# DMA crossbar transposes in place of TensorE transposes in a diffusion transformer block, with the weight loads reordered around them

## The chip, the cores and the metric

The kernel runs on one core of a Trainium2 chip. Its engines are TensorE (PE, the matrix multiplier), VectorE (DVE), ScalarE (ACT), GpSimd (POOL) and SyncE (SP). In this kernel SP only issues loads and stores, and its queue keeps the order of the program. The granted clock is the share of TensorE's full speed that the chip let it run at, as the profile records it; L681 and the like are lines of the kernel's source. The metric is the device time of one execution in microseconds (us); lower is better.

## The reference, cut to what matters

The shapes are B = 2, N = 256 tokens each, D = 1152, two heads, FC width 4608, all in bf16.

```python
h = _layernorm(x) * (1 + scale_a) + shift_a
q, k, v = ...                                   # h @ wqkv
attn = _softmax(einsum('bqhd,bkhd->bhqk', q, k) * Dh ** (-0.5))
a = einsum('bhqk,bkhd->bqhd', attn, v).reshape(B, N, D) @ wo
x = x + gate_a * a
h2 = _layernorm(x) * (1 + scale_m) + shift_m    # "LN2"
m = _gelu(h2 @ w_fc1) @ w_fc2                   # "FC1", "FC2"
return x + gate_m * m
```

The scale, shift and gate vectors, called modulation rows and gate rows below, are computed from a second input with the weights `w_mod`.

The kernel's matmuls contract over the partition axis (the 128 rows of on-chip memory). So the probabilities must be transposed before they meet V ("PV"), and the normalised rows of LN2 before they meet the FC1 weights.

## The kernel before

A small list scheduler in the kernel orders the instructions of DVE, ACT and POOL by estimated priority. PE and SP keep the order in which the program names their work.

Four buffers matter. WFC2 holds all of the FC2 weights in four quarters of nine blocks. WFC1 has four slots, so groups 4 to 8 of the FC1 weights must wait until a slot has been read. XN2, the normalised rows of LN2, lies in the last bytes of the *last* WFC2 quarter: that quarter can't be loaded until the rows have been transposed.

```python
        WFC2 = sb(O_R, 4 * W1).rearrange("p (k f) -> p k f", k=JT)
        WFC1 = [wmat(o, 512) for o in (O_A, O_A + 9216, O_C, O_C + 9216)]
...
        XN2 = [sb(O_R + 4 * W1 - (i + 1) * 2304, 2304) for i in range(4)]
```

The transposes on PE write PSUM; DVE and ACT then copy them out, those of LN2 with scale and shift applied on the way:

```python
        def pt_transposes(b, h):
            idx = b * 2 + h
            bank = s_bank[(b, h)]
            S.unit("pe", 4 * c_mm(128), "PT_%d_%d" % (b, h))
            for kjt in range(2):
                for jq in range(2):
                    tr(ps16(bank, kjt * 256 + jq * 128, 128), PP[idx][:, jq, kjt * 128:(kjt + 1) * 128], IDENT)
            copy_on("dve" if b == 0 else "act", PTS[idx].rearrange("p j k -> p (j k)"), ps16(bank, 0, 512), 512, True, "PT_ev%d" % idx)
...
        def xn2_T(t):
            b = t // 2
            xn2 = XN2[t]
            S.unit("pe", KT * c_mm(128), "xn2T_%d" % t)
            slot = [ps16(7, kt * 128, 128) if kt < 4 else ps16(6, (kt - 4) * 128, 128) for kt in range(KT)]
            for kt in range(KT):
                tr(slot[kt], xn2[:, kt * 128:(kt + 1) * 128], IDENT)
            for kt in range(KT):
                o, dst = slot[kt], H2T[:, kt, t * 128:(t + 1) * 128]
                s1, s2 = SC1M[:, kt * 2 + b:kt * 2 + b + 1], SHM[:, kt * 2 + b:kt * 2 + b + 1]
                if kt < (4 if t < 2 else 6):
                    dve(335, lambda e, o=o, dst=dst, s1=s1, s2=s2: e.tensor_scalar(out=dst, in0=o, scalar1=s1, scalar2=s2, op0=ALU.mult, op1=ALU.add),
                        [o, s1, s2], [dst], "h2T_%d_%d" % (t, kt))
                else:
                    act(440, lambda e, o=o, dst=dst, s1=s1, s2=s2: e.activation(out=dst, in_=o, func=ACTF.Identity, scale=s1, bias=s2),
                        [o, s1, s2], [dst], "h2T_%d_%d" % (t, kt))
```

This is the order of the second half. Three quarters of WFC2 are queued before PV and WO, the last one after eight FC1 half-tiles; LN2 transposes are placed between matmuls at points where their rows are ready. An FC1 tile is 128 of the 4608 columns; the first F0 = 8 tiles are done for tokens 0 to 255 and later for 256 to 511, so that FC1 can start before the last rows are there.

```python
        for q4 in range(3):
            dma(WFC2[:, 9 * q4:9 * q4 + 9, :], wfc2_v[:, 9 * q4:9 * q4 + 9, :], 9 * P * D * 2, "ld_wfc2_%d" % q4, run=2304)
        for b in range(2):
            for h in range(2):
                pv(b, h)
        wo_tile(0)
        wo_tile(1)
        wo_tile(2)
        xn2_T(0)
        wo_tile(3, {2: lambda: xn2_T(1)})
        for f in range(0, 4):
            fc1_tile(f, 0, 256)
        xn2_T(2)
        for f in range(4, F0 - 2):
            fc1_tile(f, 0, 256)
        xn2_T(3)
        for f in range(F0 - 2, F0):
            fc1_tile(f, 0, 256)
        dma(WFC2[:, 27:36, :], wfc2_v[:, 27:36, :], 9 * P * D * 2, "ld_wfc2_3", run=2304)
        for f in range(F0):
            fc1_tile(f, 256, 256)
        for f in range(F0, JT):
            if f % 4 == 0 and f // 4 >= 4:
                wfc1_load(f // 4)
            fc1_tile(f, 0, 512)
```

## Time and profile before

| | before |
|---|---|
| median of the first 3 runs | 249.41 us (249.25 to 249.88) |
| span of the profiled execution | 247.4 us |
| PE busy | 241.7 us, 98% |
| granted TensorE clock | 1.0 |
| TensorE transposes that the change removes | 52, in 8 groups |

From the profile's page: the busy times of each engine; then PE, the granted clock and the DMA engines in 40 equal slices of the span, a digit being tenths; then the chain of waits (what was running, followed back from the end) by engine.

```profile
...
PE 241.7 (98%) x1827; PEld 149.5 (60%) x1827; DVE 69.9 (28%) x179; ACT 63.8 (26%) x129; POOL 19.6 (8%) x33
...
PE   6999999999999999999999999999999999999995
...
PEclk9999999999999999999999999999999999999999
DMA  6999989999999999999953660000000000000000
...
PE 94%; ACT 2%; DMA 2%; DVE 1%; issue 0%
...
```

PE has no slack: 98% busy, 94% of the chain, full clock. The DMA engines are nearly full for 20 slices (to about 124 us), half full for four more, while the last WFC2 quarter and the later FC1 groups come, and then empty. ACT and DVE, at about a quarter each, don't limit.

From the same chain in order of time (start, length, what; `L681` is the helper for transposes in this kernel): a group of four transposes of probabilities, and three groups of nine of LN2.

```profile
...
60.40 0.22 PE psum L681 x4
...
97.14 0.52 PE psum L681 x9
...
106.72 0.50 PE psum L681 x9
...
109.19 0.57 PE psum L681 x9
...
```

They cost 0.22 us and 0.50 to 0.57 us per group and lie on the chain (of the fourth LN2 group five of the nine, 0.45 us). That is the most by which the change can shorten PE's queue: 4 × 0.22 + about 2.1 = 3.0 us, 1.2%.

The busy time of each engine by stretches (start:end and length, then busy us and count per engine; the last three columns are granted clock, DMA share, GB/s):

```profile
...
core 0: us, PE busy (x) PEld busy (x) DVE busy (x) ACT busy (x) POOL busy (x), PEclk, DMA share, GB/s
90.00:118.00 28.00, 27.91 (x238) 21.68 (x237) 17.48 (x51) 16.86 (x35) 10.26 (x13) 1.00 1.05 386
118.00:126.00 8.00, 8.00 (x46) 4.28 (x44) 0.00 (x0) 2.55 (x6) 0.00 (x0) 1.00 1.01 326
126.00:134.00 8.00, 8.00 (x39) 3.63 (x38) 0.00 (x0) 2.44 (x5) 0.00 (x0) 1.00 0.48 153
...
```

While WO, LN2 and early FC1 run (90 to 118 us) PE is busy and the loads flow beside it at 386 GB/s: the WFC2 quarters are fetched for nothing there.

### The profile page before, as it was taken

The page shows a single profiled execution, that of the slowest core. Times are in us where ns is not written, and L with a number is a line of the kernel's source. Part 1 is how long each engine was busy: PE and PEld are TensorE (multiplying, and loading weights), DVE is VectorE, ACT ScalarE, POOL GpSimd, SP SyncE. Part 2 cuts the span into 40 slices and gives each one's busy share as a digit, 9 for nine tenths or more (in the row PEclk, how much of TensorE's full clock was granted, in tenths as well). Part 3 has the DMA queues.
Part 4 walks back from the last instruction along what each step waited for, and adds up shares of the span by engine and source line. Part 5 has one row for each costly group of instructions (what it writes and reads, how often), then busy time and mean ns, then how long its engine had stood idle before and what let it go on. Part 6 is the DMA issues. An engine that isn't in the chain of part 4 may idle for free.

```text
span 247.4 us, 4146 instructions
## 1 busy us (share of the span) xinstructions
PE 241.7 (98%) x1827; PEld 149.5 (60%) x1827; DVE 69.9 (28%) x179; ACT 63.8 (26%) x129; POOL 19.6 (8%) x33
## 2 busy tenths in 40 slices
PE   6999999999999999999999999999999999999995
PEld 2589954566656766798544444444566666666674
DVE  3742440555322679950000000000012222111112
ACT  4730340344301404984333222332000000000000
POOL 1300000000013167500000000000000000000000
PEclk9999999999999999999999999999999999999999
DMA  6999989999999999999953660000000000000000
GB/s 240 372 375 393 390 299 414 426 423 420 409 385 332 309 364 391 392 386 383 358 156 138 191 191 3 0 0 0 3 16 16 19 16 16 16 19 21 27 19 17
DMA packets 27644, 51.59 MB, mean 209 GB/s; under 512 B 1511, under 2 KB 15591, under 8 KB 26475
## 3 DMA queue, kind: packets, MB, share of 16 engines
q1 hardware_dynamic: 27216, 50.14, 56.0%
q0 software_dynamic: 384, 1.19, 1.5%
q8 instruction: 14, 0.23, 0.4%
q14 instruction: 3, 0.02, 0.0%
q10 hardware_dynamic: 27, 0.00, 0.0%
HBM read 50.14 MB, written 1.19 MB: 208 GB/s over the span
## 4 chain that ended last, share of the span: by engine, by line
PE 94%; ACT 2%; DMA 2%; DVE 1%; issue 0%
PE psum L678 92%; PE psum L681 2%; DMA arena<-in_x_dram 2%; ACT arena L1049 1%; ACT arena L1033 1%; ACT arena L731 1%; ACT arena L730 1%; DVE arena L744 0%; DVE arena L783 0%; DVE arena L1139 0%; DVE arena L732 0%; DVE arena L1140 0%; DVE arena L774 0%; DVE arena L734 0%
## 5 line engine op out<-in xcount | busy, mean ns | idle before, releaser
L678 PE MATMUL psum<-arena 128*128 128x384 bf16 (+7 forms) x1720 | 237.7, 305 | 1.8 <-POOL arena L701 1.4
L678 PEld LDWEIGHTS psum<-arena 128*128 128x128 bf16 (+1 forms) x1720 | 143.8, 97 | 91.0 <-issue 3.1
L1139 DVE TENSOR_TENSOR arena<-psum,arena 128x384 f32<-128x384 f32 (+3 forms) x14 | 7.0, 501 | 119.2 <-PE psum L678 119.2
L1059 ACT ACTIVATE arena<-psum 128x512 bf16<-128x512 f32 (+1 forms) x44 | 22.5, 522 | 42.6 <-PE psum L678 42.6
L673 ACT ACTIVATE arena<-psum 128x512 bf16<-128x512 f32 (+7 forms) x29 | 15.4, 553 | 36.2 <-PE psum L678 33.8
L675 DVE CAST arena<-psum 128x512 bf16<-128x512 f32 (+4 forms) x23 | 14.0, 621 | 32.1 <-PE psum L678 32.0
L1028 POOL TENSOR_TENSOR arena<-arena 128x384 f32<-128x384 f32 x12 | 11.0, 913 | 11.2 <-DVE arena L1027 10.0
L722 DVE BATCH_NORM_STATS2 arena<-arena 128x6 f32<-128x384 f32 (+1 forms) x18 | 9.5, 548 | 0.8 <-DMA arena<-in_x_dram 0.7
L681 PE MATMUL psum<-arena 128*128 128x128 bf16 (+2 forms) x107 | 7.8, 209 | 0.9 <-DMA arena<-in_c_dram 0.7
L681 PEld LDWEIGHTS psum<-arena 128*128 128x128 bf16 (+2 forms) x107 | 6.3, 97 | 3.7 <-DMA arena<-in_c_dram 1.6
L1033 ACT ACTIVATE arena<-arena 128x1152 bf16<-128x1152 f32 x4 | 5.4, 1353 | 9.5 <-DVE arena L1032 9.5
L1027 DVE TENSOR_TENSOR arena<-psum,arena 128x384 f32<-128x384 f32 x12 | 6.6, 548 | 3.2 <-PE psum L678 2.6
L1140 DVE TENSOR_TENSOR arena<-arena 128x384 bf16<-128x384 f32 (+3 forms) x14 | 7.0, 501 | 0.5
L1049 ACT ACTIVATE arena<-psum,arena 128x128 bf16<-128x128 bf16 x16 | 6.1, 460 | 3.2 <-PE psum L681 2.5
L659 POOL DMA_DIRECT2D dit_scratch<-arena x2 | 1.2, 629 | 61.3 <-DVE arena L675 61.3
L1046 DVE TENSOR_SCALAR arena<-psum,arena 128x128 bf16<-128x128 bf16 x20 | 5.5, 338 | 2.0 <-PE psum L681 1.8
L924 ACT ACTIVATE arena<-psum,arena 128x256 bf16<-128x256 f32 x8 | 3.7, 471 | 6.9 <-PE psum L678 5.4
L726 POOL TENSOR_TENSOR arena<-arena 128x1 f32<-128x1 f32 x6 | 3.3, 553 | 8.7 <-DVE arena L725 8.7
L887 ACT ACTIVATE arena<-arena 128x256 bf16<-128x256 bf16 x6 | 2.5, 496 | 4.3 <-DVE arena L881 4.3
L920 DVE TENSOR_REDUCE arena<-psum 128x2 f32<-128x512 f32 x4 | 2.8, 690 | 1.5 <-PE psum L678 1.5
L783 DVE TENSOR_SCALAR arena<-psum,arena 128x256 bf16<-128x256 bf16 x7 | 2.4, 349 | 2.7 <-PE psum L681 1.4
L928 DVE TENSOR_TENSOR arena<-arena 128x512 bf16<-128x512 bf16 x4 | 2.8, 688 | 0.1
(37 smaller groups left out, 30.9 us busy)
## 6 DMA issues: line engine op xcount, KB each, us to landing
arena<-in_w_mod_dram SPq DMA_DIRECT2D x3, 3456.0 KB, 25.9
arena<-in_w_fc_dram SPq DMA_DIRECT2D x9, 1152.0 KB, 8.6
arena<-in_w_fc_dram SPq DMA_DIRECT2D x4, 2592.0 KB, 20.7
arena<-in_wqkv_dram SPq DMA_DIRECT2D x18, 288.0 KB, 10.0
arena<-in_w_mod_dram SPq DMA_DIRECT2D x3, 864.0 KB, 13.1
arena<-in_wqkv_dram SPq DMA_DIRECT2D x1, 2592.0 KB, 10.0
arena<-in_wo_dram SPq DMA_DIRECT2D x1, 2592.0 KB, 39.7
arena<-in_w_mod_dram SPq DMA_DIRECT2D x3, 480.0 KB, 6.8
```

The costliest lines, as they stand in the source:

```text
L673: act(c_act(n), lambda e: e.activation(out=dst, in_=src, func=ACTF.Copy), [src], [dst], name)
L675: dve(c_dve_psum16(n) if psum16 else c_dve_psum32(n), lambda e: e.tensor_copy(dst, src), [src], [dst], name)
L678: S.instr(lambda e: e.matmul(o, lhsT=l, rhs=r, start=st, stop=sp, **kw), reads=[l, r], writes=[o])
L681: S.instr(lambda e: e.transpose(o, i_, idn), reads=[i_, idn], writes=[o])
L722: dve(550, lambda e, s=s, o=o: e.bn_stats(out=o, in_=s), [s], [o], "bn_%s_%d" % (tag, ci))
L1027: dve(550, lambda e, o=o, ga=ga, x1c=x1c: e.tensor_tensor(out=x1c, in0=o, in1=ga, op=ALU.mult), [o, ga], [x1c], "wo_t1_%d_%d" % (t, ci))
L1028: S.op("pool", 930, lambda e, xs=xs, x1c=x1c: e.tensor_tensor(out=x1c, in0=x1c, in1=xs, op=ALU.add), reads=[x1c, xs], writes=[x1c], name=" ...
L1033: act(1344, lambda e: e.activation(out=xn2, in_=x1, func=ACTF.Identity, scale=rs, bias=nm), [x1, rs, nm], [xn2], "xn2_%d" % t)
L1049: act(440, lambda e, o=o, dst=dst, s1=s1, s2=s2: e.activation(out=dst, in_=o, func=ACTF.Identity, scale=s1, bias=s2), [o, s1, s2], [dst], ...
L1059: act(c_act(ntok), lambda e: e.activation(out=dst, in_=o, func=ACTF.Gelu_apprx_tanh), [o], [dst], "gelu_%d_%d" % (f, tok0))
L1139: dve(c_dve_psum32(w), lambda e, o=o, gm=gm, t1=t1: e.tensor_tensor(out=t1, in0=o, in1=gm, op=ALU.mult), [o, gm], [t1], "fc2_t1_%d_%d" % ( ...
L1140: dve(c_dve_32(w), lambda e, t1=t1, x1c=x1c, ost=ost: e.tensor_tensor(out=ost, in0=t1, in1=x1c, op=ALU.add), [t1, x1c], [ost], "fc2_out_%d ...
```

## The change

The intent: take the transposes off the engine that limits. The crossbar in the DMA path transposes bf16 from SBUF to SBUF, so PE is saved 52 transposes. PV reads the probabilities with a stride, since the crossbar's output has another order of blocks. Scale and shift are applied in place afterwards. All WFC2 loads are put behind the last LN2 transpose, which leaves the DMA engines to the transposes, and F0 grows to 12 so that FC1's first token half covers the latency of the last rows. The transposes of the probabilities are also issued earlier, ahead of most of V. The core of the diff:

```diff
-F0 = 8
+F0 = 12
...
+        def dma_T(dst, src, nbytes, name):
+            return S.op("act", 100.0, lambda e: e.dma_start_transpose(dst, src), ...)
...
         def pt_transposes(b, h):
-            (4 TensorE transposes, then a copy out of PSUM)
+            dma_T(PTS[idx].rearrange("p j k q -> p (j k) q"), PP[idx].rearrange("p j k -> p (j k)"), P * 1024, "PT_%d" % idx)
...
         def xn2_T(t):
-            (9 TensorE transposes, then 9 scaled copies out of PSUM)
+            dma_T(H2T[:, :, tok], XN2[t], P * D * 2, "xn2T_%d" % t)
+            (9 scalings in place, 6 on DVE and 3 on ACT)
...
-        for q4 in range(3):
-            dma(WFC2[:, 9 * q4:9 * q4 + 9, :], ...)
         for b in range(2):
             for h in range(2):
                 pv(b, h)
-        wo_tile(0)
-        wo_tile(1)
-        wo_tile(2)
-        xn2_T(0)
-        wo_tile(3, {2: lambda: xn2_T(1)})
-        (FC1 half-tiles, with xn2_T(2) and xn2_T(3) among them)
-        dma(WFC2[:, 27:36, :], ...)
+        for t in range(4):
+            wo_tile(t)
+            xn2_T(t)
+        for q4 in (3, 0, 1, 2):
+            dma(WFC2[:, 9 * q4:9 * q4 + 9, :], ...)
+        for f in range(F0):
+            fc1_tile(f, 0, 256)
         for f in range(F0):
             fc1_tile(f, 256, 256)
```

More of the change, by code (lines that the diff above doesn't have):

```diff
@@ L610, in build_kernel @@
         PP = [sb(O_P + i * 1024, 1024).rearrange("p (j k) -> p j k", j=2) for i in range(4)]
-        PTS = [sb(O_PT + i * 1024, 1024).rearrange("p (j k) -> p j k", j=2) for i in range(4)]
+        PTS = [sb(O_PT + i * 1024, 1024).rearrange("p (j k q) -> p j k q", j=2, k=2) for i in range(4)]
         GA = [sb(O_GA + b * 2304, 2304) for b in range(2)]
@@ L660, in dma @@
                         name=name, dma_bytes=nbytes * eff, is_out=is_out)
+        def dma_T(dst, src, nbytes, name):
+            return S.op("act", 100.0, lambda e: e.dma_start_transpose(dst, src), reads=[src], writes=[dst], name=name, dma_bytes=nbytes)
         def dve(cost, fn, reads, writes, name):
@@ L931, in pt_transposes @@
             idx = b * 2 + h
-            bank = s_bank[(b, h)]
-            S.unit("pe", 4 * c_mm(128), "PT_%d_%d" % (b, h))
-            for kjt in range(2):
-                for jq in range(2):
-                    tr(ps16(bank, kjt * 256 + jq * 128, 128), PP[idx][:, jq, kjt * 128:(kjt + 1) * 128], IDENT)
-            copy_on("dve" if b == 0 else "act", PTS[idx].rearrange("p j k -> p (j k)"), ps16(bank, 0, 512), 512, True, "PT_ev%d" % idx)
+            dma_T(PTS[idx].rearrange("p j k q -> p (j k) q"), PP[idx].rearrange("p j k -> p (j k)"), P * 1024, "PT_%d" % idx)
         v_banks = [0, 1, 2]
@@ L992, in pv @@
                 for kjt in range(2):
-                    mm(ps32(PVB[b][q], half * 256, 256), V[:, 2 * b + kjt, g * 128:(g + 1) * 128], PTS[idx][:, kjt, :], kjt == 0, kjt == 1)
+                    mm(ps32(PVB[b][q], half * 256, 256).rearrange("p (j q) -> p j q", j=2), V[:, 2 * b + kjt, g * 128:(g + 1) * 128],
+                       PTS[idx][:, :, kjt, :], kjt == 0, kjt == 1)
             tok = slice(b * 256, (b + 1) * 256)
@@ L1013, in acc_bank, with wo_tile @@
             return b
-        def wo_tile(t, before={}):
+        def wo_tile(t):
             b = t // 2
             for ci in range(NCH):
-                if ci in before:
-                    before[ci]()
                 S.unit("pe", KT * c_mm(CH), "wo_%d_%d" % (t, ci))
@@ L1036, in xn2_T @@
             b = t // 2
-            xn2 = XN2[t]
-            S.unit("pe", KT * c_mm(128), "xn2T_%d" % t)
-            slot = [ps16(7, kt * 128, 128) if kt < 4 else ps16(6, (kt - 4) * 128, 128) for kt in range(KT)]
+            tok = slice(t * 128, (t + 1) * 128)
+            dma_T(H2T[:, :, tok], XN2[t], P * D * 2, "xn2T_%d" % t)
             for kt in range(KT):
-                tr(slot[kt], xn2[:, kt * 128:(kt + 1) * 128], IDENT)
-            for kt in range(KT):
-                o, dst = slot[kt], H2T[:, kt, t * 128:(t + 1) * 128]
+                h = H2T[:, kt, tok]
                 s1, s2 = SC1M[:, kt * 2 + b:kt * 2 + b + 1], SHM[:, kt * 2 + b:kt * 2 + b + 1]
-                if kt < (4 if t < 2 else 6):
-                    dve(335, lambda e, o=o, dst=dst, s1=s1, s2=s2: e.tensor_scalar(out=dst, in0=o, scalar1=s1, scalar2=s2, op0=ALU.mult, op1=ALU.add),
-                        [o, s1, s2], [dst], "h2T_%d_%d" % (t, kt))
-                else:
-                    act(440, lambda e, o=o, dst=dst, s1=s1, s2=s2: e.activation(out=dst, in_=o, func=ACTF.Identity, scale=s1, bias=s2),
-                        [o, s1, s2], [dst], "h2T_%d_%d" % (t, kt))
+                if kt % 3 < 2:
+                    dve(180, lambda e, h=h, s1=s1, s2=s2: e.tensor_scalar(out=h, in0=h, scalar1=s1, scalar2=s2, op0=ALU.mult, op1=ALU.add),
+                        [h, s1, s2], [h], "h2T_%d_%d" % (t, kt))
+                else:
+                    act(440, lambda e, h=h, s1=s1, s2=s2: e.activation(out=h, in_=h, func=ACTF.Identity, scale=s1, bias=s2),
+                        [h, s1, s2], [h], "h2T_%d_%d" % (t, kt))
         def fc1_tile(f, tok0, ntok):
@@ L1077, in build_kernel @@
         s_and_softmax(1, 1)
+        for b in range(2):
+            for h in range(2):
+                pt_transposes(b, h)
         v_proj(0, 2)
-        pt_transposes(0, 0)
-        v_proj(1, 0)
-        pt_transposes(1, 0)
-        v_proj(1, 1)
-        pt_transposes(0, 1)
-        v_proj(1, 2)
-        pt_transposes(1, 1)
+        for ci in range(NCH):
+            v_proj(1, ci)
         v_proj(2, 0)
@@ L1098, in build_kernel @@
         wfc1_load(3)
-        for q4 in range(3):
-            dma(WFC2[:, 9 * q4:9 * q4 + 9, :], wfc2_v[:, 9 * q4:9 * q4 + 9, :], 9 * P * D * 2, "ld_wfc2_%d" % q4, run=2304)
         for b in range(2):
@@ L1103, in build_kernel @@
                 pv(b, h)
-        wo_tile(0)
-        wo_tile(1)
-        wo_tile(2)
-        xn2_T(0)
-        wo_tile(3, {2: lambda: xn2_T(1)})
-        for f in range(0, 4):
-            fc1_tile(f, 0, 256)
-        xn2_T(2)
-        for f in range(4, F0 - 2):
-            fc1_tile(f, 0, 256)
-        xn2_T(3)
-        for f in range(F0 - 2, F0):
-            fc1_tile(f, 0, 256)
-        dma(WFC2[:, 27:36, :], wfc2_v[:, 27:36, :], 9 * P * D * 2, "ld_wfc2_3", run=2304)
+        for t in range(4):
+            wo_tile(t)
+            xn2_T(t)
+        for q4 in (3, 0, 1, 2):
+            dma(WFC2[:, 9 * q4:9 * q4 + 9, :], wfc2_v[:, 9 * q4:9 * q4 + 9, :], 9 * P * D * 2, "ld_wfc2_%d" % q4, run=2304)
+        for f in range(F0):
+            fc1_tile(f, 0, 256)
         for f in range(F0):
@@ L1147, in build_kernel @@
             sems = {e: es.enter_context(nc.semaphore("c_" + e)) for e in ENGINES}
-            dma_sems = [es.enter_context(nc.semaphore("d%d" % i)) for i in range(56)]
+            dma_sems = [es.enter_context(nc.semaphore("d%d" % i)) for i in range(64)]
+            S.n_other_dma_sems = 16
             S.emit(nc, block, sems, dma_sems)
```

## The prediction

> **What bounds the kernel now.** TensorE. The busy table has PE at 98% of the 247.4 us span, the chain of waits is 94% PE, and the granted clock is 1.0 throughout. Only what shortens PE's queue, without making PE wait, shortens the run.
>
> **What goes.** 52 TensorE transposes: 16 of the probabilities, 36 of the LN2 output. In the chain the former cost 0.22 us per group of four (0.88 us), the latter 0.50 to 0.57 us per group of nine (2.1 us). In all 3.0 us of PE, on the chain, 1.2%. Evictions go too, but ACT (26%) and DVE (28%) are not the limit.
>
> **What comes.** Eight crossbar transposes on ACT's DMA queue. No trace here has one. The Trainium skill, "DMA: Bandwidth & Descriptors", section "Latency and other measured facts", gives 261 GB/s for a less favourable transpose; with that page's fixed cost of about 2 us, 295 KB are estimated at 3.1 us from issue to landing.
>
> - Probabilities: softmax ends near 63 us and PV starts near 80 us (timeline). Even at 8 us beside the bulk loads (the gate loads took 8.2 us) they are hidden.
> - LN2: in the timeline, LN2 takes 7.3 us from the eviction of a tile's last WO piece to the normalised row. FC1's first tile needs WO tile 1, which ends two WO tiles (8.8 us) before FC1. With 7 us LN2, 3 us transpose and 1 to 2 us scaling, FC1 starts some 3 us late, near 103.5 us. The gain is spent there.
>
> **What moves, and decides.** All four quarters of WFC2 (10.6 MB) now follow the LN2 transposes: the first of them overwrites the normalised rows, so SP waits for the last transpose, and the loads of FC1's weight groups 4 to 8 stand behind in SP's order. In before three quarters were under way during WO and early FC1 (380 to 392 GB/s from 90 to 118 us, windows); group 4 was needed at FC1 tile 16, near 135 us. In the new ACT order the last transpose stands behind the activation table load and the Gelus of FC1 tiles 0 to 3: I put its issue at 109 to 111 us, its landing at 112 to 114. Then 10.6 MB at 390 GB/s (27.2 us), 1.18 MB for group 4 (3.2 us) and 2 us of latency: group 4 lands at 145 to 147 us. PE reaches tile 16 at 103.5 + 24×0.98 + 4×1.94 = 135 us and stands for 10 to 12 us. The end moves by 146 − 135 = 11 us. After such a pause the clock gate may be cold: at the start of the trace 14 wide matmuls took 356 ns each against 217 later ("TensorE: Matmul & The Clock Gate", Part 1, says the same of idle PE): about 2 us more. F0 = 12 itself costs nothing (1.96 against 1.94 us per tile).
>
> **Prediction.** 262 us, 255.5 to 270. Chances: faster 0.02, same 0.05, slower 0.93.
>
> **What would show it.** PE's waits: about 3 us at FC1's start, on DVE or ACT scaling; about 11 us in FC1 near 135 us, released by the DMA of in_w_fc. DMA share near zero from about 90 to 113 us, then full to about 147 us. PE busy down by 3 us.
>
> **What would make it wrong.** Transposes of 6 us or more push it towards 270; at 2 us it is near 259. If the ACT queue blocks while issuing, evictions stall PE earlier. If loads run faster than 390 GB/s the pause shrinks.

## The result, and the profile after

| | before | after |
|---|---|---|
| median of 4 runs each | 249.64 us | 265.38 us (264.93 to 265.94) |
| ratio | | 1.063, 95% interval 1.0599 to 1.0661 |
| span of the profiled execution | 247.4 us | 263.2 us |
| PE busy | 241.7 us (98%) | 243.1 us (92%) |
| mean granted clock | 1.0 | 0.966 |

Ratios here and below are the mean time of one kernel's fast runs over that of the other's of the same rounds, so they are not quite the ratio of the medians quoted. All outputs are right.

The same lines of the page, after, and the chain by line (in every kernel with a crossbar transpose `L681` is the helper for matmuls and `L684` that for transposes):

```profile
...
PE 243.1 (92%) x1802; PEld 151.0 (57%) x1811; DVE 69.1 (26%) x181; ACT 62.4 (24%) x127; POOL 19.6 (7%) x33
...
PE   6999999999999995999990499999999999999995
...
PEclk9999999999999999799996589999999999999999
DMA  7999989999999962279999985000000000000010
...
PE 71%; DMA 22%; DVE 3%; ACT 1%; POOL 1%; SPq 1%; issue 0%
PE psum L681 70%; DMA arena<-in_w_mod_dram 13%; DMA arena<-in_w_fc_dram 7%; DMA arena<-in_x_dram 2%; PE psum L684 1%; DVE arena L1040 1%; POOL arena L1025 1%; SPq L659 1%; DVE arena L1024 1%; DVE arena L725 1%; ACT arena L733 0%; ACT arena L734 0%; DVE arena L1029 0%; DVE arena L747 0%; DVE arena L786 0%
...
```

PE now has two holes, around the 16th and the 22nd slice, and the clock dips behind each. The DMA engines are at two tenths in slices 16 and 17, where they were full before, and the loading that filled this time now comes after it. DMA now makes up 22% of the chain. This line needs care: the 13% for `in_w_mod` is a load that landed just in time at 69.4 us and cost PE 0.9 us at most; the 7% for `in_w_fc` is the real one.

What PE waited for (total, times, longest; start-up waits left out, `L1040` is the scaling of the LN2 rows):

```profile
...
PE psum L681 <- DMA arena<-in_w_fc_dram: 10.7, 1, 10.7
PE psum L681 <- DVE arena L1040: 3.1, 1, 3.1
...
```

The chain in order of time around them:

```profile
...
103.81 0.23 DVE arena L1040
...
104.08 24.56 PE psum L681 x205
128.64 19.58 DMA arena<-in_w_fc_dram
...
148.35 5.63 PE psum L681 x14
...
```

The stretches (columns as before):

```profile
...
95.00:104.00 9.00, 6.00 (x37) 3.42 (x35) 8.16 (x24) 3.97 (x8) 5.86 (x8) 1.00 0.35 68
104.00:114.00 10.00, 9.92 (x73) 7.70 (x74) 3.04 (x17) 6.76 (x13) 0.55 (x1) 0.83 0.31 59
...
128.00:138.00 10.00, 9.57 (x52) 4.94 (x51) 0.00 (x0) 3.21 (x7) 0.00 (x0) 1.00 1.05 391
138.00:148.30 10.30, 0.00 (x0) 0.00 (x0) 0.00 (x0) 0.26 (x1) 0.00 (x0) 0.58 1.08 370
148.30:152.00 3.70, 3.65 (x9) 1.34 (x10) 0.00 (x0) 0.00 (x0) 0.00 (x0) 0.50 1.10 348
152.00:156.00 4.00, 3.95 (x16) 1.64 (x16) 0.00 (x0) 1.19 (x2) 0.00 (x0) 0.83 1.10 348
...
```

Between 95 and 114 us the DMA engines are a third busy, with transposes alone. From 138.0 to 148.3 us PE does nothing at all, and then runs at half clock for the 3.7 us shown and part of the next 4 us.

The crossbar transposes of LN2, as ACT issued them (start, time on the issuing queue), with the load of the Gelu table that falls between:

```profile
...
95.24 1.26 ACTq L663 DMA_TRANSPOSE arena<-arena  x1
...
99.63 1.31 ACTq L663 DMA_TRANSPOSE arena<-arena  x1
...
106.71 1.28 ACT L1053 ACT_TABLE_LOAD   x1
...
109.26 1.30 ACTq L663 DMA_TRANSPOSE arena<-arena  x1
...
110.64 1.35 ACTq L663 DMA_TRANSPOSE arena<-arena  x1
...
```

In the trace's own queries each of these four took 3.2 to 3.3 us from issue to landing. Over all eight transposes (minimum, median, maximum):

```profile
...
DMA to landing us min/median/max: 3.2/9.2/17.9
```

The four of the probabilities, issued beside the bulk loads, are the long ones: 15.1 to 17.9 us.

SP's wait for a transpose, and its issues of WFC2's four quarters (start, time on the queue):

```profile
...
SPq L474 <- DMA arena<-arena: 27.7, 1, 27.7
...
114.06 14.54 SPq L659 DMA_DIRECT2D arena<-in_w_fc_dram  x4
...
```

The sequence in the trace after is thus: ACT issues the last transpose at 110.6 us; it lands at 113.9; SP, which had been waiting for it for 27.7 us, issues WFC2 from 114.06 us on; behind 10.6 MB comes FC1 group 4; it lands at 148.2 us. PE was ready for it at 148.35 − 10.73 = 137.6 us. The records of the DMA packets show the order too: those of WFC2 (2304 bytes each) start from 115.1 to 144.2 us, and the first of the FC1 groups behind them (1024 bytes) at 142.6 us.

### The profile page after: what moved, and what is told of

The parts are those of the page before. It is cut to its first block, busy times and chain, and to the rows that moved or that the text cites. A ratio compares the mean times of both kernels' runs of the same rounds, so it can differ in the third digit from the quotient of the medians.

```text
span 263.2 us, 4112 instructions
## 1 busy us (share of the span) xinstructions
PE 243.1 (92%) x1802; PEld 151.0 (57%) x1811; DVE 69.1 (26%) x181; ACT 62.4 (24%) x127; POOL 19.6 (7%) x33
## 4 chain that ended last, share of the span: by engine, by line
PE 71%; DMA 22%; DVE 3%; ACT 1%; POOL 1%; SPq 1%; issue 0%
PE psum L681 70%; DMA arena<-in_w_mod_dram 13%; DMA arena<-in_w_fc_dram 7%; DMA arena<-in_x_dram 2%; PE psum L684 1%; DVE arena L1040 1%; POOL arena L1025 1%; SPq L659 1%; DVE arena L1024 1%; DVE arena L725 1%; ACT arena L733 0%; ACT arena L734 0%; DVE arena L1029 0%; DVE arena L747 0%; DVE arena L786 0%
## 5 line engine op out<-in xcount | busy, mean ns | idle before, releaser
L681 PE MATMUL psum<-arena 128*128 128x384 bf16 (+7 forms) x1747 | 240.9, 305 | 16.1 <-DMA arena<-in_w_fc_dram 10.7
L681 PEld LDWEIGHTS psum<-arena 128*128 128x128 bf16 (+1 forms) x1756 | 148.4, 98 | 106.3 <-issue 17.2
L1053 ACT ACTIVATE arena<-psum 128x256 bf16<-128x256 f32 (+1 forms) x48 | 23.1, 489 | 56.0 <-PE psum L681 56.0
L678 DVE CAST arena<-psum 128x512 bf16<-128x512 f32 (+4 forms) x23 | 14.0, 621 | 33.6 <-PE psum L681 33.4
L676 ACT ACTIVATE arena<-psum 128x512 bf16<-128x512 f32 (+6 forms) x27 | 14.2, 550 | 36.3 <-PE psum L681 36.3
L1025 POOL TENSOR_TENSOR arena<-arena 128x384 f32<-128x384 f32 x12 | 10.9, 912 | 10.7 <-DVE arena L1024 10.0
L1040 DVE TENSOR_SCALAR arena<-arena 128x128 bf16<-128x128 bf16 x24 | 6.0, 322 | 6.3 <-DMA arena<-arena 6.3
L1043 ACT ACTIVATE arena<-arena 128x128 bf16<-128x128 bf16 x12 | 5.0, 483 | 2.0 <-ACT arena L1043 1.0
L684 PEld LDWEIGHTS psum<-arena 128*128 128x128 bf16 (+2 forms) x55 | 2.7, 96 | 2.8 <-DMA arena<-in_c_dram 1.7
L684 PE MATMUL psum<-arena 128*128 128x128 bf16 (+2 forms) x55 | 3.4, 199 | 1.0 <-DMA arena<-in_c_dram 0.8
```

The source lines that it names most:

```text
L676: act(c_act(n), lambda e: e.activation(out=dst, in_=src, func=ACTF.Copy), [src], [dst], name)
L678: dve(c_dve_psum16(n) if psum16 else c_dve_psum32(n), lambda e: e.tensor_copy(dst, src), [src], [dst], name)
L681: S.instr(lambda e: e.matmul(o, lhsT=l, rhs=r, start=st, stop=sp, **kw), reads=[l, r], writes=[o])
L684: S.instr(lambda e: e.transpose(o, i_, idn), reads=[i_, idn], writes=[o])
L1025: S.op("pool", 930, lambda e, xs=xs, x1c=x1c: e.tensor_tensor(out=x1c, in0=x1c, in1=xs, op=ALU.add), reads=[x1c, xs], writes=[x1c], name=" ...
L1040: dve(180, lambda e, h=h, s1=s1, s2=s2: e.tensor_scalar(out=h, in0=h, scalar1=s1, scalar2=s2, op0=ALU.mult, op1=ALU.add), [h, s1, s2], [h] ...
```

## The experiments

**The theory.** The transposes are cheap. What costs is the queue order that came with them: all of WFC2 waits for the last transpose, and the FC1 groups wait behind WFC2. From that follow the 10.7 us pause and the half clock after it. **Rival 1**: the crossbar transposes themselves cost it, by late rows and a blocked ACT queue. **Rival 2**: holding the loads back was needless, and transposes would run as well beside them.

The runs in four groups (e1 to e4, e5 to e8, e9 and e10, e11 and e12), with the median of the kernel before in the same rounds. Each group ran on another chip, so across groups the ratios compare better than the times:

| run | what | us | before | ratio (95%) |
|---|---|---|---|---|
| e1_order | after, other load order | 251.75 | 249.49 | 1.0073 (1.0047 to 1.0099) |
| e2_before_late | before, with late loads | 261.02 | 249.49 | 1.0455 (1.0439 to 1.0472) |
| e3_early_loads | after, with early loads | 267.52 | 249.49 | 1.0721 (1.0705 to 1.0738) |
| e4_pt_only | before, crossbar for probabilities only | 249.20 | 249.49 | 0.9986 (0.9973 to 0.9998) |
| e5_fill_pause | after, dummy matmuls in the long pause | 262.91 | 249.60 | 1.0528 (1.0514 to 1.0541) |
| e6_fill_start | e1, dummy matmuls in the wait at FC1's start | 250.25 | 249.60 | 1.0018 (1.0005 to 1.0031) |
| e7_mix | crossbar where its latency is hidden | 249.94 | 249.60 | 1.0008 (0.9993 to 1.0023) |
| e8_mix_rows | e7, one V tile moved | 249.75 | 249.60 | 1.0004 (0.9988 to 1.0021) |
| e9_mix_sp | e8, transposes issued by SP, loads interleaved | 249.41 | 249.61 | 0.9988 (0.9976 to 1.0000) |
| e10_mix_sp_no_pt | e9 with probabilities on TensorE | 249.69 | 249.61 | 1.0021 (0.9985 to 1.0057) |
| e11_mix_order | e9, group 7 one place earlier | **248.13** | 249.60 | 0.9930 (0.9916 to 0.9943) |
| e12_pt_rows | e4, one V tile moved | 249.34 | 249.60 | 0.9985 (0.9971 to 0.9998) |

### Only the load order (e1_order)

```diff
-        for q4 in (3, 0, 1, 2):
+        for q4 in (3, 0):
             dma(WFC2[:, 9 * q4:9 * q4 + 9, :], ...)
...
+        wfc1_load(4)
+        wfc1_load(5)
+        (WFC2 quarter 1)
+        wfc1_load(6)
+        (WFC2 quarter 2)
         for f in range(F0, JT):
-            if f % 4 == 0 and f // 4 >= 4:
+            if f % 4 == 0 and f // 4 >= 7:
                 wfc1_load(f // 4)
```

> All eight crossbar transposes stay; only the order of SP's weight loads changes (WFC2 quarters 3 and 0, then FC1 groups 4 and 5, then quarter 1, group 6, quarter 2). My theory (the queue of loads behind the last transpose makes the 10.7 us pause and the cold clock after it): the pause at FC1 tile 16 goes, FC1 still starts near 104 us after a wait of about 3 us, and the time is 251.5 to 253 us. The rival (the transposes themselves cost it: late rows, a blocked ACT queue): no better than 262 us.

Measured: 251.75 us. In its trace PE has one wait in FC1 left, the one at its start:

```profile
...
PE psum L681 <- DVE arena L1040: 3.1, 1, 3.1
...
```

All eight crossbar transposes are still there, and 265.38 − 251.75 = 13.6 of the 15.7 us are gone. Rival 1 falls as the main cause; the transposes, F0 = 12 and the scaling in place, which all stay in e1, can account for the 2 us that are left (e6 comes back to them).

### Only the late loads (e2_before_late)

```diff
-        for q4 in range(3):
-            dma(WFC2[:, 9 * q4:9 * q4 + 9, :], ...)
...
         xn2_T(3)
+        for q4 in (3, 0, 1, 2):
+            dma(WFC2[:, 9 * q4:9 * q4 + 9, :], ...)
...
-        dma(WFC2[:, 27:36, :], ...)
```

> The kernel before with all its TensorE transposes; only the four WFC2 loads are moved behind the last LN2 transpose, in the order 3, 0, 1, 2, ahead of FC1 groups 4 to 8. My theory: the last row is read at about 110 us, group 4 lands some 34 us later, near 144 us, PE needs it at 135 us, waits 9 us and restarts cold: 259.5 to 262 us. The rival (crossbar transposes cost it): 249.5 us, as before.

Measured: 261.02 us, with not one crossbar transpose in the kernel. Its only new wait (`L678` is the helper for matmuls there, as in the kernel before):

```profile
...
PE psum L678 <- DMA arena<-in_w_fc_dram: 9.3, 1, 9.3
...
```

This is the other half of the proof: the load order alone makes 11.5 us. It is less than in the changed kernel for two reasons that the traces show. TensorE's last transpose has read its row at 110.1 us, 4.0 us before SP goes on in the changed kernel, and group 4 lands at 144.6 us against 148.2. And PE runs at half clock for 2.9 us after the pause, against 5.0 us. Half of the 2.1 us between these, added to the 3.6 us, is the difference of the two profiled spans, 263.2 − 258.5 = 4.7 us.

### Early loads beside the transposes (e3_early_loads)

```diff
-        for q4 in (3, 0, 1, 2):
+        for q4 in (0, 1, 2, 3):
```

With this order the first three quarters don't wait for anything, so they flow during WO and LN2 as in the kernel before.

> The changed kernel with WFC2 quarters 0, 1, 2 queued first, as in the kernel before, and quarter 3 last, so that the LN2 transposes run beside 8 MB of loads. If a transpose beside loads takes what the probabilities' did (15 to 18 us against 3.2 us in the quiet queue), tile 0's lands near 110 us, tile 1's a few us later, FC1 starts near 114 us, the pause at FC1 tile 16 is gone, and the time is 259 to 264 us, no gain. If transposes don't mind the loads, FC1 starts near 104 us and the time is 251 to 253 us, and holding the loads back was needless.

Measured: 267.52 us, worse than the change itself, and above the range that I gave. The pause for FC1 weights is gone, but FC1 starts at 119.8 us, after a wait of 19 us:

```profile
...
PE psum L681 <- DVE arena L1040: 19.0, 1, 19.0
...
```

The issues of the first two LN2 transposes:

```profile
...
95.10 1.89 ACTq L663 DMA_TRANSPOSE arena<-arena  x1
...
108.34 1.96 ACTq L663 DMA_TRANSPOSE arena<-arena  x1
...
```

The first took 13.2 us from issue to landing and the second 11.1, against 3.2 in the quiet queue. My estimate missed that the second can't be issued until ACT, which keeps its order, has done its share of scaling with the first, so that both latencies add up. The records of the DMA packets show where the time goes. The transpose of one tile is 1152 packets of 256 bytes. Alone they pass in 1.55 us, from 1.2 us after the issue. Here the first tile's started 3.9 us after the issue and took from 99.0 to 107.5 us, while 1192 packets of 2304 bytes from the loads passed: about one for one. It is so in nearly every single microsecond, and when the loads run out at 117 us, 437 packets of the second tile pass within one. The probabilities' transposes in the changed kernel agree: 2048 of their packets passed beside 2132 of the loads. This fits what the Trainium skill states in "DMA: Bandwidth & Descriptors", section "Queues, rings and completion order": an engine alternates between the queues that have work, packet by packet. (That the profile's packets are the packets of that page is not shown.) With turns of 256 against 2304 bytes the transpose gets a tenth of the bytes, here 35 of 361 GB/s. Rival 2 falls too.

### Only the probabilities (e4_pt_only)

The kernel before, with the transposes of the probabilities (their place in the order too) and PV as in the change and nothing else.

> The kernel before with only the probabilities transposed by the crossbar. In the changed kernel this took 0.88 us off PE's queue but PE then waited for the modulation weights, whose load lands at 69.4 us, and reached the transposes of the modulation rows only 0.5 us earlier. LN2 of WO tile 1 is just in time before FC1 in the kernel before, so even that may be lost there. Theory: 248.8 to 249.6 us, same as before. Rival (the probabilities' transposes, 15 to 18 us late and blocking ACT for up to 4.5 us, hold up V or PV): 251 us or more.

Measured: 249.20 us, 0.14% less, just clear of zero. The four transposes land at 69.3, 74.3, 77.9 and 80.0 us in the changed kernel's trace (issue plus time to landing), and no engine is seen waiting for them. ACT's queue was held for up to 4.5 us while issuing, also without a wait of PE behind it. Of the 0.88 us of PE work saved, about a third shows in the time; the interval allows 0.05 to 0.67 us.

### The clock after the long pause (e5_fill_pause)

```diff
+            if f == 16:
+                for i in range(45):
+                    (dummy matmul 128x512 into PSUM bank 7, which nobody reads)
             fc1_tile(f, 0, 512)
```

> The changed kernel with 45 dummy matmuls (128x512, an unused PSUM bank, 9.7 us at full clock) queued on TensorE just ahead of FC1 tile 16, inside the pause. They compute nothing that is used. If the cold clock after the pause costs what its records say (0.50 of full speed for the first 3.7 us, 0.83 over the next 4), this takes about 2.4 us off although PE has more to do: 262.7 to 263.4 us. If the pause is the whole cost and the clock a side show: 265.4 us, or a little more.

Measured: 262.91 us. PE has 9.7 us more to do and the kernel is 2.5 us faster. The stretch of the pause and the one after it, to be read against the two lines above:

```profile
...
138.00:148.30 10.30, 9.31 (x43) 4.04 (x42) 0.00 (x0) 0.29 (x1) 0.00 (x0) 1.00 1.08 370
148.30:152.00 3.70, 3.65 (x17) 1.69 (x18) 0.00 (x0) 0.60 (x1) 0.00 (x0) 1.00 1.10 347
...
```

The weights land at the same time as before; the clock stays at 1.00. So the half clock after the pause costs 265.38 − 262.91 = 2.5 us. The clock records agree: in the changed kernel half clock holds for 5.0 us of PE's work after the pause, and half of that is 2.5 us.

### The clock at FC1's start (e6_fill_start)

The same device on e1: 13 dummy matmuls (2.8 us) ahead of FC1's first tile.

> The run with the new load order (251.75 us), with 13 dummy matmuls (2.8 us) queued ahead of FC1's first tile, inside its 3.1 us wait for the rows of WO tile 1. Theory: the wait stays, the cold clock after it goes, 1.5 to 1.8 us less: 249.9 to 250.4 us, so that what is left of the change's cost is less than 1 us. If the clock is not what the new order still loses: 251.7 us.

Measured: 250.25 us, 1.5 us less than e1. There is independent support in e1's own runs: three of the four had a mean clock of 0.993 and took 251.66 to 251.92 us; the fourth had a clock of 1.0 and took 250.29. A wait of 3.1 us is thus short enough to be forgiven sometimes (one of the four was traced, so that the fourth had the same wait is assumed).

### A version with the crossbar only where its latency is hidden (e7 to e12)

The first half of FC1 needs the rows of WO tiles 0 and 1 at once, the second half those of tiles 2 and 3 more than 10 us later. So I left tiles 0 and 1 on TensorE, gave tiles 2 and 3 and the probabilities to the crossbar, kept e1's load order, and set F0 to 14.

> A try for the best of both: the crossbar for the probabilities and for rows of WO tiles 2 and 3 only, whose latency lies behind FC1's first token half (F0 = 14); TensorE for tiles 0 and 1, whose rows FC1 waits for; WFC2 behind the last transpose but in the order of the first experiment. Theory: no wait above 0.5 us on PE in FC1; PE saves 1.0 us after FC1's start and about 0.3 us before: 247.9 to 248.6 us, 0.4 to 0.6% under the kernel before. If held loads cost anything by themselves: 250 us or more.

Measured: 249.94 us, a miss. The trace shows FC1 groups landing late, a wait that I had put at nothing (two waits, the longer 1.3 us, for group 4):

```profile
...
PE psum L681 <- DMA arena<-in_w_fc_dram: 1.6, 2, 1.3
...
```

It also names a wait of PE's weight loads on a Gelu (`L1072`), which I took for a second cost, a PSUM bank freed late:

```profile
...
PEld psum L681 <- ACT arena L1072: 1.8, 1, 1.8
...
```

I put it down to ACT's queue: two transposes issued back to back hold it, and the Gelus stand behind them.

```profile
...
108.41 3.14 ACTq L663 DMA_TRANSPOSE arena<-arena  x2
111.60 1.21 ACT L1072 ACTIVATE arena<-psum 128x256 bf16<-128x256 f32 x4 [2.81 <-PE psum L681]
...
```

The traces do not bear this out. From 104 to 116 us, around the held queue, PE is busy for 12.00 of 12 us. The weight loads' wait lies elsewhere, from 133.4 to 135.2 us, over the wait for group 4 (133.9 to 135.2 us): it is the same stall, and the Gelu that the profile names had ended at 134.5 us.

> The same with one more V tile ahead of the modulation rows on PE, so that PE has work while their weights land at 69.4 us. Theory: the 0.4 us wait on in_w_mod goes, the gate rows land about 1 us later, LN2 of tile 1 bounds FC1's start: within 0.3 us of the run above, either way. If the rows' wait were all that hid the gain: 0.4 us under it.

Measured: 249.75 us, the same as e7 within the noise. e8 moves one V tile ahead of the modulation rows, nothing else. For e9, still reading e7 in the first way, I let SP, which has nothing to do there, issue the two transposes, and put each FC1 group between two WFC2 quarters:

```diff
-            dma_T(H2T[:, :, tok], XN2[t], P * D * 2, "xn2T_%d" % t)
+            dma_T(H2T[:, :, tok], XN2[t], P * D * 2, "xn2T_%d" % t, "sp")
...
-        (WFC2 3, 0, FC1 4, 5, WFC2 1, FC1 6, WFC2 2, FC1 7, 8)
+        (WFC2 3, FC1 4, WFC2 0, FC1 5, WFC2 1, FC1 6, WFC2 2, FC1 7, 8)
```

> The mixed kernel with the extra V tile (249.75 us), mended where its trace shows waits: the two LN2 transposes are issued by SP, so ACT is not held 3.1 us and the Gelus free their PSUM banks in time; each FC1 group is queued between two WFC2 quarters (3, group 4, 0, 5, 1, 6, 2, 7, 8), so group 4 no longer shares the queue with three others. Theory: the 1.1 us of waits on in_w_fc and some 1 us of bank waiting go: 247.4 to 248.3 us, 0.5 to 0.9% under the kernel before. If the gain is lost to something that these two don't touch: 249 us or more.

Measured: 249.41 us, again a miss. The wait for group 4 is gone, but now group 7, which stands behind quarter 2, comes late:

```profile
...
PE psum L681 <- DMA arena<-in_w_fc_dram: 1.2, 1, 1.2
...
PEld psum L681 <- ACT arena L1072: 1.6, 1, 1.6
...
```

The wait on `L1072` is there as well, though ACT issues none of these transposes now, and it has moved to 157 us with the late group (156.5 to 158.2 us). So the issuing engine was not what e7 and e8 lost their gain to. The late groups account for it by the sum, 249.94 − 1.6 = 248.3 us for e7 and 249.41 − 1.2 = 248.2 us for e9; e11 below, in which no group is late, took 248.13 us. What issuing from SP is worth by itself was not tested.

> The same, but with the probabilities transposed on TensorE and V as in the kernel before: the crossbar is left for rows of WO tiles 2 and 3 alone. Theory: PE saves only the 1.07 us of their transposes: 248.2 to 248.8 us, 0.2 to 0.8 us above the run with both.

Measured: 249.69 us, with an interval too wide (one of its six runs had a clock of 0.991 and took 252.43 us; that run's trace was not kept) to say what the probabilities contribute here. It is inconclusive. Moving group 7 ahead of quarter 2, which FC2 reads only some 15 us later, was the last step:

> The mixed kernel whose transposes SP issues (249.41 us), with FC1 group 7 moved ahead of WFC2 quarter 2, which is first read some 15 us later. Its trace shows one wait on in_w_fc, 1.2 us at 157 us, for that group. Theory: the wait goes and nothing takes its place: 248.0 to 248.5 us, 0.4 to 0.6% under the kernel before. If the gain is lost elsewhere: 249.2 us or more.

Measured: 248.13 us, 0.7% under the kernel before (interval 0.6 to 0.8%, clear of zero) and as expected. In its trace PE waits for no weights and no rows in FC1, and its busy time is 2.1 us below the kernel before:

```profile
...
PE 239.6 (97%) x1839; PEld 152.9 (62%) x1847; DVE 68.1 (28%) x177; ACT 63.5 (26%) x133; POOL 19.6 (8%) x33
...
```

This is the fastest version seen, faster than both kernels. From e9 to e11 one load changed its place, which is worth 1.3 us (1.4 by the ratios).

> The kernel with only the probabilities on the crossbar (249.20 us), with one more V tile ahead of the modulation rows on PE, so that PE does not wait for their weights (a 0.5 us wait of its weight loads on in_w_mod). Theory: the rest of the 0.88 us comes back unless the gate rows, now about 1 us later, hold up WO's eviction: 248.7 to 249.2 us.

Measured: 249.34 us against 249.20 for e4 (other rounds, ratios 0.9985 and 0.9986). The weight loads' wait on in_w_mod is gone from the trace, and the time is not better; where the rest of the 0.88 us went stays open.

## Why the prediction was right

It said 262 us, 255.5 to 270; measured were 265.38. Point by point:

- **Removed work.** 3.0 us of PE that can't be kept: right in kind. FC1 started at 104.08 us (103.5 predicted) after a wait of 3.1 us (3 predicted) on the scaling by DVE.
- **A transpose of LN2.** Estimated at 3.1 us from the skill's page, whose fixed 2 us were fitted to DMAs that GpSimd issues and not ACT; measured 3.2 to 3.3 in the quiet queue. The estimate was right in the sum, not in its parts, and so partly by luck: the packets alone took 1.55 us for 295 KB, which is about 190 GB/s rather than 261, and the rest 1.7 us rather than 2.
- **The last transpose.** Issue predicted at 109 to 111 us, landing at 112 to 114; measured 110.6 and 113.9.
- **Group 4's landing.** Predicted 145 to 147 us, measured 148.2. From 114 to 148.3 us the stretches add up to 6.0 × 272 + 8.0 × 395 + 10 × 391 + 10.3 × 370 GB/s = 12.5 MB, while WFC2 and group 4 are 11.8 MB. So about 0.7 MB, 2 us of loading, belonged to later groups, which I had not counted (the packet records have 663 packets of 1024 bytes more than group 4's 1152 in this time).
- **The pause.** Predicted 10 to 12 us near 135 us, released by in_w_fc; measured 10.7 us from 137.6 us. e1 and e2 show that the load order makes it. That its length fits so well is partly luck: both its start (135 us predicted) and its end (146 us) came over 2 us later.
- **The clock.** Predicted at about 2 us after the pause; e5 measures 2.5. I missed that the 3 us wait at FC1's start would trip the clock as well: 1.5 us by e6. But that was not simply added to the end of the changed kernel: group 4's landing set the end, and reaching tile 16 later only made the pause shorter.
- **PE busy down by 3 us**: wrong. It went up by 1.4 us, because matmuls at half clock count as busy for about twice the time (from 148.3 to 152 us 9 matmuls kept PE busy for 3.65 us at half clock, 17 in e5 at full clock). Where the clock stayed up (e11), busy time fell.
- **The probabilities.** I allowed 8 us beside the loads; they took 15.1 to 17.9. They were still hidden, with little to spare: the last landed at 80.0 us, and PV ran from about 79 to 83.5 us.
- **DMA share near zero from 90 to 113 us**: wrong in size. It was 1.00 from 90 to 95 us, as earlier loads were still coming in, and then a third, which is the transposes' own traffic.
- **The sum.** Group 4 landed at 148.35 − 135.1 = 13.2 us later than the kernel before began tile 16 (135.1 us from its chain: 90 half-size matmuls of 0.109 us after 109.77, then eight tiles of 1.94); with 2.5 us of clock that is 15.7 us, and 265.38 − 249.64 = 15.7. I had 11 + 2. The 3 us that were short are mostly the landing, at 148.35 us where I had reckoned with 146, and half a microsecond of clock.

What stays open: about 0.5 us that e6 is still slower than before (0.65 by the medians, 0.18% by the ratio), and the part of e4's saving that does not reach the end.

## What to carry to other kernels

When work is moved from a busy engine to the DMA queues, first ask what must now wait for the new transfer, and what stands behind that in an in-order queue; here 3 us of saved matrix work cost 15.7 us, of which a change of load order alone gave 13.6 back. A transpose by crossbar has a latency, short in a quiet queue (3.2 us here) and several times longer beside bulk loads (11.1 and 13.2 us in e3), so it belongs where a stage of other work covers it, and queued loads should be sorted by when they are first read. A pause of the matrix engine can cost the slow clock after it besides its own length: 2.5 us here after 10.7 us, 1.5 us after most waits of 3.1 us, nothing after the 1.3 us of e7, whose clock stayed at 1.0. Dummy matmuls in the pause tell the two apart. And a wait that the profile names should be placed in time before it is believed: e7's second wait was the first one seen by another queue.

## What the Trainium skill lacked or had wrong

- "DMA: Bandwidth & Descriptors", section "Latency and other measured facts", and "Advanced Engine Details and Errata", section "X-Bar Transpose (TRN2)" (as fast as regular DMAs, 350 to 400 GB/s; the first gives 261 with a non-contiguous middle dimension): the transposes of 295 KB here passed in 1.55 us, about 190 GB/s, and took 3.2 to 3.3 us from issue to landing, while plain loads ran at 386 GB/s. Two back to back reached 197 GB/s.
- No page gives a transpose's time beside bulk loads: 13.2 and 11.1 us for 295 KB in e3, 15.1 to 17.9 us for 131 KB of probabilities. The packet-by-packet turns that "DMA: Bandwidth & Descriptors" describes fit the rate in e3 (1152 packets of 256 bytes beside 1192 of 2304); no page draws that conclusion for small packets.
- No page says for trn2 by name how long issuing a transpose holds the engine that issues it ("DMA: Bandwidth & Descriptors" has cycle counts for trn3 and for unnamed earlier generations): 1.3 us on ACT in the quiet queue, up to 4.5 us beside bulk loads.
- "TensorE: Matmul & The Clock Gate", Part 1, names an idle window of about 3.4 us. Here a wait of 3.1 us, shorter than that, cost the clock in three of e1's four runs and not in the fourth; the price was 1.5 us, and 2.5 us after the 10.7 us pause.
